# The second matrix of an attention + ELU layer: seven products of halves in its last three blocks

## The chip, the cores and the metric

The kernel runs on one core of one Trainium2 chip. The metric is the device time in microseconds (us) of one execution. The times given are the median of several runs and their lowest and highest; the profile is of one more execution, taken by the hardware profiler.

## The reference

Attention on two scales comes first, and then a two-layer block with an ELU between the layers:

```python
# q, k, v: (8, 8, 576, 64) = batch, heads, sequence, head size
out_up    = np.repeat(attention over q, k, v averaged over 4 positions, 4)
out_local = attention over q, k, v with the mask abs(i - j) < 4
x = (out_up + out_local).transpose(0, 2, 1, 3).reshape(4608, 512)
...
h = x @ w_in                                   # (4608, 512) @ (512, 2048)
g = np.where(h > 0, h, np.exp(np.minimum(h, 0)) - 1)
return g @ w_out                               # (4608, 2048) @ (2048, 512), float32
```

Inputs and output are float32; the operands of the matmuls are fp16, the sums in PSUM float32.

## The kernel before, in words

**Blocks and batches.** The 4608 tokens are cut into nine blocks `t` of 512 (`TBLK`); the attention runs over eight batches `b` of 576 tokens, four pairs of heads `j` in each. Block 6 holds tokens of batches 5 and 6, block 7 tokens of batches 6 and 7 (64 of the last), block 8 the rest of batch 7. The attention of the last batch is computed while blocks 5 and 6 run in the first layer.

**First layer.** `mm1(t, fc)` makes one of 16 pieces of 128 hidden columns: four matmuls of 128x128 weights by 512 tokens into a PSUM buffer `hp` (two buffers), an exponential on ScalarE into `e`, then two instructions on VectorE: a TENSOR_SCALAR in place on `e` (minimum with 1, minus 1) and a SCALAR_TENSOR_TENSOR that adds max(`hp`, 0) and writes the piece of `gt`. `gt` has two buffers, each [128, 16, 512].

**Second layer.** `mm2(t, i)`, 16 steps: for each 128 tokens, 16 matmuls (four per step) of a 128x128 piece of `gt` as weights by 512 columns of `WO` into a PSUM buffer `op`; after the fourth step a copy on ScalarE into `os` and a DMA to the output. The last 128 tokens are done in two pieces, 384 and 128 columns.

**Attention.** `pair_transposes(b, j)`: transposes on TensorE, a copy to `qt` on ScalarE, and `sums`: on GpSimd two additions, `t` and then `qd` (queries summed over four positions). `pair_scores` needs `qd`. `normalise(b, j, lg)`: two multiplications on VectorE into `ln` (two buffers), and one addition per block on GpSimd into `xt(t)`, the input of `mm1`. Before each pair GpSimd casts q, k and v.

**Order.** It is written out by hand: every piece of work is put into a list by `at(time, function, ...)`; the list is sorted by time and issued in that order, and each engine works through its own instructions in the order of issue. The times are numbers in tables in units of one step. `mm1_at(t, i)` gives step i of block t's first layer; from block 3 on `mm2_at(t, i)` is `mm1_at(t + 1, 0) + 0.5 + i`, so each step of the first layer of a block is followed by one step of the second layer of the block before, and after the last step of block 8 the second layer of block 8 stands alone. `LAST` holds the places of the last batch's attention, relative to the start of block 7.

**Memory.** All SBUF tiles belong to one pool `sb` that lives to the end.

## Time and profile before

| | us |
|---|---|
| median of 3 runs (lowest to highest) | 351.59 (348.52 to 353.46) |
| span of the profiled execution, its own time | 353.6 |
| block 6: first matmul of its first layer to that of block 7 | 249.15 to 281.46 |
| block 7: to the first matmul of block 8 | 281.46 to 309.09 |
| block 8's first layer, to its last matmul's end | 309.09 to 335.85 |
| the matmuls behind it | 335.85 to 350.73 |

The profile gives the busy time of each engine (PE is TensorE, PEld its weight loads, DVE VectorE, ACT ScalarE, POOL GpSimd, SP the queue of DMAs), and each instruction with its line in the kernel, its start in the span and its length. "x4" stands for four instructions of one kind merged into one row. Behind a "<-" in square brackets stands what ended the idle time of the engine before the row. For a difference of one or two per cent the stretch in which the changed instructions stand has to be read, not the sums over the span.

### The profile page before, as it was taken

The page shows a single profiled execution, that of the slowest core. Times are in us where ns is not written, and L with a number is a line of the kernel's source. Part 1 is how long each engine was busy: PE and PEld are TensorE (multiplying, and loading weights), DVE is VectorE, ACT ScalarE, POOL GpSimd, SP SyncE. Part 2 cuts the span into 40 slices and gives each one's busy share as a digit, 9 for nine tenths or more (in the row PEclk, how much of TensorE's full clock was granted, in tenths as well). Part 3 has the DMA queues.
Part 4 walks back from the last instruction along what each step waited for, and adds up shares of the span by engine and source line. Part 5 has one row for each costly group of instructions (what it writes and reads, how often), then busy time and mean ns, then how long its engine had stood idle before and what let it go on. Part 6 is the DMA issues. An engine that isn't in the chain of part 4 may idle for free.

```text
span 353.6 us, 10486 instructions
## 1 busy us (share of the span) xinstructions
PE 335.8 (95%) x4288; PEld 185.3 (52%) x4288; DVE 236.2 (67%) x466; ACT 180.6 (51%) x312; POOL 160.0 (45%) x298
## 2 busy tenths in 40 slices
PE   8897998899889998899999999999999999999996
PEld 4665784455455544445555555545455544444443
DVE  2316999665878775977797789779756955555510
ACT  3572795256665653466355636663553444444421
POOL 4563458286875841973396449755300600000000
PEclk9998999879989999999999999999999999999999
DMA  9999997899998869898979797953014010010012
GB/s 177 201 209 192 213 208 152 200 213 190 188 185 158 167 139 181 168 190 158 196 150 214 158 214 155 168 131 54 30 35 116 32 59 31 32 52 37 32 59 89
DMA packets 98768, 48.89 MB, mean 138 GB/s; under 512 B 81617, under 2 KB 93217, under 8 KB 98721
## 3 DMA queue, kind: packets, MB, share of 16 engines
q1 hardware_dynamic: 94417, 41.86, 58.7%
q0 software_dynamic: 4064, 6.26, 10.0%
q8 instruction: 33, 0.54, 0.7%
q10 hardware_dynamic: 240, 0.11, 0.2%
q14 instruction: 14, 0.11, 0.1%
HBM read 41.97 MB, written 9.55 MB: 146 GB/s over the span
## 4 chain that ended last, share of the span: by engine, by line
PE 75%; DVE 13%; DMA 6%; issue 3%; ACT 3%; SPq 0%; DVEq 0%; ACTq 0%
PE op L739 31%; PE hp L719 28%; DVE gt L725 4%; DMA rcb<-rd 3%; DVE e L724 3%; DVE ln L671 2%; DMA rd<-rc 2%; PE sc L758 2%; PE tqk L328 2%; PE sc L458 2%; PE lg L602 1%; ACT e L723 1%; PE vs L405 1%; PE lg L622 1%; PE den L518 1%
## 5 line engine op out<-in xcount | busy, mean ns | idle before, releaser
L739 PE MATMUL op<-WO,gt 128*128 128x512 f16 (+2 forms) x592 | 146.0, 375 | 0.5 <-DVE gt L725 0.5
L723 ACT ACTIVATE e<-hp 128x512 f16<-128x512 f32 x144 | 86.2, 599 | 107.1 <-PE hp L719 95.3
L719 PE MATMUL hp<-xt,WI 128*128 128x512 f16 x512 | 133.7, 385 | 1.4 <-DVE gt L725 1.3
L725 DVE SCALAR_TENSOR_TENSOR gt<-hp,e 128x512 f16<-128x512 f32 x144 | 99.6, 692 | 6.4
L724 DVE TENSOR_SCALAR e<-e 128x512 f16<-128x512 f16 x144 | 60.6, 421 | 58.4 <-ACT e L723 58.0
L739 PEld LDWEIGHTS <-gt 128*128 128x128 f16 x592 | 55.4, 98 | 61.7 <-issue 1.6
L719 PEld LDWEIGHTS <-WI 128*128 128x128 f16 x512 | 55.6, 115 | 50.0 <-issue 3.2
L683 POOL TENSOR_TENSOR xt<-ln 128x128 f16<-128x128 f16 (+7 forms) x55 | 36.6, 693 | 56.9 <-DVE ln L671 56.9
L481 ACT ACTIVATE pex<-sc 128x580 f16<-128x580 f32 (+1 forms) x56 | 30.1, 594 | 9.2 <-PE sc L471 8.6
L302 POOL CAST v<-v 128x640 f16<-128x640 f32 (+1 forms) x32 | 23.7, 741 | 20.4 <-DMA v<-in_v_dram 13.6
L394 POOL TENSOR_TENSOR t<-qt 128x288 f32<-128x288 f16 x27 | 18.1, 670 | 31.4 <-ACT qt L358 31.4
L745 ACT COPY os<-op 128x512 f32<-128x512 f32 (+2 forms) x37 | 21.4, 578 | 18.9 <-PE op L739 18.8
L377 DVE TENSOR_REDUCE ke<-kt 128x145 f16<-128x580 f16 x28 | 21.0, 751 | 2.4 <-ACT kt L365 2.4
L358 ACT COPY qt<-tqk 128x576 f16<-128x576 f16 x28 | 17.9, 639 | 8.4 <-PE tqk L328 7.7
L671 DVE TENSOR_TENSOR ln<-lg,rcb 128x580 f16<-128x580 f32 x28 | 21.1, 752 | 0.0
L241 POOL CAST k<-k 96x768 f16<-96x768 f32 x24 | 19.8, 825 | 0.1
L241 POOL CAST q<-q 96x768 f16<-96x768 f32 x24 | 19.6, 818 | 0.0
L698 PE MATMUL hp<-xt,WI 128*128 128x256 f16 x128 | 17.0, 283 | 0.7 <-DVE v L276 0.4
L496 DVE TENSOR_TENSOR pex<-pex,MASK 128x580 f16<-128x580 f16 x28 | 13.6, 486 | 3.0 <-ACT pex L481 2.8
L698 PEld LDWEIGHTS <-WI 128*128 128x128 f16 x128 | 13.3, 116 | 1.9 <-issue 0.8
L396 POOL TENSOR_TENSOR qd<-t 128x144 f16<-128x144 f32 x27 | 12.1, 448 | 2.1
L458 PEld LDWEIGHTS <-kt 64*64 64x64 f16 x560 | 6.9, 109 | 11.2 <-issue 8.6
(113 smaller groups left out, 273.4 us busy)
## 6 DMA issues: line engine op xcount, KB each, us to landing
out_dram<-os SPq DMA_DIRECT2D x35, 256.0 KB, 2.1
v<-in_v_dram SPq DMA_DIRECT2D x111, 80.0 KB, 4.5
q<-in_q_dram SPq DMA_DIRECT2D x25, 288.0 KB, 3.9
...
```

Source lines behind the costliest of these rows:

```text
L241: nc.gpsimd.tensor_copy(out=x[:], in_=src)
L302: nc.gpsimd.tensor_copy(out=v16[:], in_=v32[:].rearrange("p (e c) d -> p c e d", e=2))
L481: nc.scalar.activation(out=s["p"][:, :, a : a + n], in_=g2(sc, a, n), func=AF.Exp, scale=SCALE / 16 if a else SCALE,)
L671: nc.vector.tensor_tensor(out=ln[:, 0 : 2 * WL].rearrange("p (m h u) -> p m h u", h=2, u=WQ), in0=_free(lg[:, 0:1], [[WQ, WM], [512, 2], [ ...
L683: eng.tensor_tensor(out=xt(t)[:, j, t0 - TBLK * t : t1 - TBLK * t], in0=ln[:, a:z], in1=_rep4(ln[:, ga : ga + (z - a) // 4]), op=AB.add,)
L698: nc.tensor.matmul(FS[i][:, 256 * f : 256 * f + 256], w_in(dc, 2 * n + f), xts[0][:, dc, 256 * h : 256 * h + 256], start=(f == dc == 0), s ...
L719: nc.tensor.matmul(hp, w_in(dc, fc), xts[t][:, dc, :], start=(dc == 0), stop=(dc == DMC - 1),)
L723: nc.scalar.activation(out=e, in_=hp, func=AF.Exp)
L724: nc.vector.tensor_scalar(out=e, in0=e, scalar1=1.0, scalar2=-1.0, op0=AB.min, op1=AB.add)
L725: nc.vector.scalar_tensor_tensor(out=to, in0=hp, scalar=0.0, op0=AB.max, in1=e, op1=AB.add)
L739: nc.tensor.matmul(op_[:, a:z], gts[t][:, fc, 128 * tt : 128 * tt + 128], WO[:, fc, a:z], start=(fc == 0), stop=(fc == FCN - 1),)
L745: nc.scalar.copy(out=os_[:, a:z], in_=op_[:, a:z])
```

## The change

For blocks 6, 7 and 8 (`SW = 6`) the second layer is computed in Strassen's form (Winograd's variant). Of `gt`, the tokens are halved (first and last 256) and the hidden columns (first and last 1024), which gives quarters a11, a12, a21, a22; of `WO`, the hidden rows and the output columns, b11 to b22. Seven products of quarters take the place of eight:

- four differences of quarters of `WO`, kept in a tile `T` [128, 4, 8, 256]: `weights_7(n, c)`, 16 subtractions on GpSimd, each of 128x512 elements, once;
- for each block four sums of quarters of `gt`: `sums_7(t, g)`, four groups g of four operations of 128x512 on GpSimd, a group after every fourth step of the first layer (in block 8 the last group is on VectorE). One of them, a11 - a21, is written over a21; the three others go into a tile `S`;
- `product(t, u, n)`, n from 1 to 7, for each unit u of 2 x 128 tokens (128 of the first half and 128 of the last): eight matmuls of 256 columns, each with its own 128x128 weights. Both units together have 112 matmuls of 256 columns, where `mm2` had 64 of 512. Partial results are copied to `sn` by ScalarE, and added on VectorE into `ou` (behind product 4 a [128, 2, 256] addition, behind product 5 one of [128, 256]).

The first layer of these blocks takes the hidden columns in another order (0, 8, 1, 9, ...), so that each group of sums finds its four pieces. In the slots between the steps of blocks 7 and 8 stand products at steps 0 to 5 and 7, and at 8 to 13 and 15: steps 6 and 14 have none behind them. In block 8 all products stand behind the last step.

```diff
-    def mm1(t, fc):
+    def mm1(t, i):
+        fc = i if t < SW else i // 2 + 8 * (i % 2)
...
+    def weights_7(n, c):
+        T, k = W7["T"], slice(2 * c, 2 * c + 2)
+        b11, b12 = WO[:, k, 0:MH], WO[:, k, MH:DM]
...
+        x, y = ((b12, b11), (b22, T[:, 0, k]), (b22, b12), (b21, T[:, 1, k]))[n]
+        nc.gpsimd.tensor_tensor(out=T[:, n, k], in0=x, in1=y, op=AB.subtract)
+    def sums_7(t, g):
...
+        a11, a12, a21, a22 = G[:, k, 0:TH], G[:, l, 0:TH], G[:, k, TH:TBLK], G[:, l, TH:TBLK]
+        eng = nc.vector if (t, g) == (NT - 1, 3) else nc.gpsimd
+        for to, x, y, op in (
+            (S[:, 0, k], a21, a22, AB.add), (a21, a11, a21, AB.subtract),
+            (S[:, 1, k], S[:, 0, k], a11, AB.subtract), (S[:, 2, k], a12, S[:, 1, k], AB.subtract),
+        ):
+            eng.tensor_tensor(out=to, in0=x, in1=y, op=op)
...
+    def product(t, u, n, k0=0, k1=FH):
+        xz, y, sn, ou = unit(t, u)
...
+        to = y[:, 0:MH] if n in (1, 3, 5, 6) else xz[:, 0:MH] if n == 2 else xz[:, MH:DM]
+        for k in range(k0, k1):
+            w, x = (
+                (G[:, k, a], WO[:, k, 0:MH]), (G[:, FH + k, a], WO[:, FH + k, 0:MH]),
+                (S[:, 2, k, a], WO[:, FH + k, MH:DM]), (G[:, FH + k, b], T[:, 3, k]),
+                (S[:, 0, k, a], T[:, 0, k]), (S[:, 1, k, a], T[:, 1, k]), (G[:, k, b], T[:, 2, k]),
+            )[n - 1]
+            nc.tensor.matmul(
+                to, w, x, start=(k == 0 and n in (1, 2)), stop=(k == FH - 1),
...
+        if n in (1, 6, 7):
+            nc.scalar.copy(out=sn[:, {1: 0, 6: 1, 7: 2}[n], :], in_=to)
+        if n == 4:
+            nc.vector.tensor_tensor(
+                out=ou[:, :, 0:MH], in0=xz[:].rearrange("p (c m) -> p c m", c=2), in1=sn[:, 0:2, :],
+                op=AB.add,
+            )
+        if n == 5:
+            nc.vector.tensor_tensor(out=ou[:, 1, MH:DM], in0=to, in1=sn[:, 2, :], op=AB.add)
+            nc.sync.dma_start(out=out[z : z + 128], in_=ou[:, 1, :])
...
+        if n == 3:
+            nc.scalar.copy(out=ou[:, 0, MH:DM], in_=to)
...
-            if 16 * t + i <= 16 * NT - 4:
+            if t < SW:
                 at(mm2_at(t, i), mm2, t, i)
+    at(PLAN[B - 1]["cast"][3] + 0.05, close_feed)
+    at(PLAN[B - 1]["tr"][3] + 0.05, close_turn)
+    for n in range(4):
+        for c in range(4):
+            at(PLAN[B - 1]["cast"][3] + 0.6 + 1.2 * (4 * n + c), weights_7, n, c)
+    for t in range(SW, NT):
+        for g in range(4):
+            at(mm1_at(t, 4 * g + 3) + 0.05, sums_7, t, g)
+        z = mm2_at(t, 0)
+        if t < NT - 1:
+            for u in range(2):
+                for n, x in zip((1, 2, 7, 6, 4, 5, 3), (0, 1, 2, 3, 4, 5, 7)):
+                    at(z + 8 * u + x, product, t, u, n)
+        else:
+            steps = [(u, n, 0, FH - 1) for u in range(2) for n in (1, 2)]
+            steps += [(u, n, FH - 1, FH) for u in range(2) for n in (1, 2)]
+            steps += [(u, n) for u, n in ((0, 7), (0, 6), (1, 7), (1, 6), (0, 4), (0, 5), (1, 4), (1, 5), (0, 3), (1, 3))]
+            for n, x in enumerate(steps):
+                at(z + n, product, t, *x)
```

For room, tiles that only the attention uses go into two pools of their own (`lo` and `tu`), which are closed after the last batch's casts and after its last transposes; `T`, `S`, `sn` and `ou` take their places. A line of the kernel up to the second layer stands six or seven lines further down than before.

How GpSimd's own row of instructions changes is seen at two places. The first lies at the start of block 6, on GpSimd (POOL): the additions into `xt` of batch 6, and `t` and `qd` of the last two pairs of batch 7. Before:

```order
L683 TENSOR_TENSOR xt<-ln 128x128
L683 TENSOR_TENSOR xt<-ln 128x448
L394 TENSOR_TENSOR t_5455<-qt 128x288
L396 TENSOR_TENSOR qd<-t_5455 128x144
L394 TENSOR_TENSOR t_5549<-qt 128x288
L396 TENSOR_TENSOR qd<-t_5549 128x144
```

After, where `w_5276` is the tile `T` of weight differences:

```order
L772 TENSOR_TENSOR w_5276<-WO 128x512
L689 TENSOR_TENSOR xt<-ln 128x128
L689 TENSOR_TENSOR xt<-ln 128x448
L689 TENSOR_TENSOR xt<-ln 128x128
L689 TENSOR_TENSOR xt<-ln 128x448
L772 TENSOR_TENSOR w_5276<-WO 128x512 x2
L400 TENSOR_TENSOR t_5469<-qt 128x288
L402 TENSOR_TENSOR qd<-t_5469 128x144
L772 TENSOR_TENSOR w_5276<-WO 128x512
L772 TENSOR_TENSOR w_5276<-WO,w_5276 128x512
L400 TENSOR_TENSOR t_5565<-qt 128x288
L402 TENSOR_TENSOR qd<-t_5565 128x144
```

One weight difference now stands ahead of the second half of batch 6's additions, two ahead of the first `t` and two ahead of the second.

The second place is the end of block 6, again on GpSimd: from the last pair's `qd` to the additions into `xt` of batch 7, whose 64-wide ones write block 7's input. Before:

```order
L394 TENSOR_TENSOR t_5549<-qt 128x288
L396 TENSOR_TENSOR qd<-t_5549 128x144
L683 TENSOR_TENSOR xt<-ln 128x64
L683 TENSOR_TENSOR xt<-ln 128x512
L683 TENSOR_TENSOR xt<-ln 128x64
L683 TENSOR_TENSOR xt<-ln 128x512
```

After, the last twelve rows up to the second half of these additions (`s_5597` is the tile `S` of block 6):

```order
L772 TENSOR_TENSOR w_5276<-WO 128x512 x2
L772 TENSOR_TENSOR w_5276<-WO,w_5276 128x512
L785 TENSOR_TENSOR s_5597<-gt 128x512
L785 TENSOR_TENSOR gt<-gt 128x2x256
L785 TENSOR_TENSOR s_5597<-s_5597,gt 128x512
L785 TENSOR_TENSOR s_5597<-gt,s_5597 128x512
L689 TENSOR_TENSOR xt<-ln 128x64
L689 TENSOR_TENSOR xt<-ln 128x512
L689 TENSOR_TENSOR xt<-ln 128x64
L689 TENSOR_TENSOR xt<-ln 128x512
L772 TENSOR_TENSOR w_5276<-WO,w_5276 128x512 x2
L689 TENSOR_TENSOR xt<-ln 128x64
```

Between `qd` and the first of these additions stand eight weight differences (two, three and three) and three groups of sums now, each group behind the step of the first layer that it needs; two more differences stand between the two halves of the additions.

The third place is VectorE in block 7, at its steps 4 to 6. Before, only the pairs of the first layer stand there (with the tiles' numbers, since the rows read alike without them):

```order
L724 TENSOR_SCALAR e_6076<-e_6076 128x512
L725 SCALAR_TENSOR_TENSOR gt_6019<-hp_6077,e_6076 128x512
L724 TENSOR_SCALAR e_6090<-e_6090 128x512
L725 SCALAR_TENSOR_TENSOR gt_6019<-hp_6091,e_6090 128x512
L724 TENSOR_SCALAR e_6103<-e_6103 128x512
L725 SCALAR_TENSOR_TENSOR gt_6019<-hp_6104,e_6103 128x512
```

After:

```order
L731 TENSOR_SCALAR e_6148<-e_6148 128x512
L732 SCALAR_TENSOR_TENSOR gt_6067<-hp_6149,e_6148 128x512
L817 TENSOR_TENSOR ou_6080<-xz_6077,sn_6079 128x2x256
L731 TENSOR_SCALAR e_6166<-e_6166 128x512
L732 SCALAR_TENSOR_TENSOR gt_6067<-hp_6167,e_6166 128x512
L822 TENSOR_TENSOR ou_6080<-y_6078,sn_6079 128x256
L731 TENSOR_SCALAR e_6185<-e_6185 128x512
L732 SCALAR_TENSOR_TENSOR gt_6067<-hp_6186,e_6185 128x512
```

The additions of products 4 and 5 now stand behind the pairs of steps 4 and 5.

More of the change, by code (lines that the diff above doesn't have):

```diff
@@ L35 @@
 FLIP = 3
+SW = 6
 I1 = 31
@@ L120, in const @@
     def const(a, name, queue):
-        t = C[name] = sb.tile(list(a.shape), FP16, tag=name, bufs=1, name=name)
+        pool = sb if name in ("ID", "MASK", "IND2", "VR2") else lo
+        t = C[name] = pool.tile(list(a.shape), FP16, tag=name, bufs=1, name=name)
         queue.dma_start(out=t[:], in_=nc.inline_tensor(a, name=name + "c").ap())
+    feed = ctx.enter_context(ExitStack())
+    turn = ctx.enter_context(ExitStack())
+    lo = feed.enter_context(tc.tile_pool(name="lo", bufs=1, side="right"))
+    tu = turn.enter_context(tc.tile_pool(name="tu", bufs=1))
     front = ctx.enter_context(ExitStack())
@@ L175, in load_wo @@
         nc.gpsimd.dma_start(out=WO[:, 4 * n : 4 * n + 4, :], in_=src)
[L177 removed]
+    KD = [lo.tile([128, 2 * KG + 16], FP16, tag=f"kd{i}", bufs=1, name="kd") for i in range(4)]
     KE = [sb.tile([128, 192], FP16, tag=f"ke{i}", bufs=1, name="ke") for i in range(4)]
@@ L391, in sums @@
         else:
-            t2 = sb.tile([128, 2 * SD], FP32, tag="pex", bufs=2, name="t2")
+            t2 = tu.tile([128, 2 * SD], FP32, tag="pex", bufs=2, name="t2")
             at_ = src.rearrange("p (g f) -> p f g", f=2)
@@ L730, in mm2 @@
         tt, part = i // 4, i % 4
-        cols = ((0, DM),)
-        if t == NT - 1 and tt == 3:
-            cols, part = ((0, 384), (384, DM)), 0
-        for a, z in cols:
-            if part == 0:
-                ops[(t, tt)] = bank("misc", "op")
-            op_ = ops[(t, tt)]
-            for fc in range(4 * part, 4 * part + 4 if len(cols) == 1 else FCN):
-                nc.tensor.matmul(
-                    op_[:, a:z], gts[t][:, fc, 128 * tt : 128 * tt + 128], WO[:, fc, a:z],
-                    start=(fc == 0), stop=(fc == FCN - 1),
-                )
-            if part == 3 or len(cols) == 2:
-                os_ = sb.tile([128, DM], FP32, tag="os", bufs=3, name="os")
-                nc.scalar.copy(out=os_[:, a:z], in_=op_[:, a:z])
-                r = TBLK * t + 128 * tt
-                nc.sync.dma_start(out=out[r : r + 128, a:z], in_=os_[:, a:z])
+        if part == 0:
+            ops[(t, tt)] = bank("misc", "op")
@@ new lines, in mm2 @@
+        op_ = ops[(t, tt)]
+        for fc in range(4 * part, 4 * part + 4):
+            nc.tensor.matmul(
+                op_[:], gts[t][:, fc, 128 * tt : 128 * tt + 128], WO[:, fc, :],
+                start=(fc == 0), stop=(fc == FCN - 1),
+            )
+        if part == 3:
+            os_ = sb.tile([128, DM], FP32, tag="os", bufs=3, name="os")
+            nc.scalar.copy(out=os_[:], in_=op_[:])
+            r = TBLK * t + 128 * tt
+            nc.sync.dma_start(out=out[r : r + 128], in_=os_[:])
```

58 lines of the change are left out of this document (45 added, 13 removed).

## The prediction

> Times are microseconds from the start of the span; i counts the 16 steps of a block's first layer, each followed by one step of the second layer of the block before. "Matmul step" is one such group of four matmuls.
>
> **What bounds the kernel now.** The page comes first: which engine is full.
>
> ```profile
> PE 335.8 (95%) x4288; PEld 185.3 (52%) x4288; DVE 236.2 (67%) x466; ACT 180.6 (51%) x312; POOL 160.0 (45%) x298
> ```
>
> An average over stages says little, so the stretches of blocks 6, 7, 8 and of the last second layer were asked for; columns after the length are busy PE, PEld, DVE, ACT, POOL, then the granted clock.
>
> ```profile
> 249.15:281.46 32.31, 32.31 (x391) 16.61 (x390) 22.59 (x46) 15.47 (x26) 6.34 (x10) 1.00 0.20 58
> 281.46:309.09 27.63, 27.63 (x129) 13.49 (x128) 15.87 (x33) 11.91 (x20) 0.20 (x1) 1.00 0.10 39
> 309.09:335.85 26.76, 26.76 (x125) 13.06 (x124) 15.62 (x32) 11.31 (x19) 0.00 (x0) 1.00 0.10 40
> 335.85:353.57 17.72, 14.88 (x85) 7.54 (x83) 1.11 (x3) 3.69 (x7) 0.00 (x0) 1.00 0.20 74
> ```
>
> PE is full in all of them, at full clock; GpSimd is nearly idle (6.34 of 32.31, then nothing), VectorE is busy 22.59 of 32.31 in block 6 and 15.87 of 27.63 in block 7. The chain of work that ended last consists there of matmuls alone, four at a time:
>
> ```profile
> 335.15 0.86 PE hp L719 x4
> 336.02 14.73 PE op L739 x84
> 350.81 0.27 ACT os L745
> ```
>
> So 0.86 per four is 216 ns per matmul of 512 columns, and any matmul taken away shortens the end, unless PE waits for something instead. That something can only be an engine that gets new work: GpSimd or VectorE.
>
> **The change, part by part.**
>
> *Fewer columns.* A block's second layer was 64 matmuls of 512 columns, 64 x 0.216 = 13.8. It becomes 7 products x 2 units x 8 = 112 matmuls of 256 columns, each with its own 128x128 weight load. The first layer of block 0 already runs that form:
>
> ```profile
> 44.26 2.81 PE L698 MATMUL hp<-xt,WI 128*128 128x256 f16 x24
> L698 PE MATMUL hp<-xt,WI 128*128 128x256 f16 x128 | 17.0, 283 | 0.7 <-DVE v L276 0.4 <-DVE gt L725 0.3
> ```
>
> 24 in 2.81, the last of them 0.28 long: (2.81 - 0.28) / 23 = 110 ns, half of 216; weight loads stay hidden there. 112 x 0.110 = 12.3, so 1.5 less per block. This falls in block 7's slots (second layer of block 6), in block 8's, and in the tail. The tail is 84 matmuls, 14.73; it becomes 15 products of 0.88 = 13.2, 1.5 less. The last copy grows from 128 columns to 256, and the last group's sums stand on VectorE:
>
> ```profile
> L745 ACT COPY os<-op 128x512 f32<-128x512 f32 x35 | 20.6, 590 | 16.5 <-PE op L739 16.4
> L496 DVE TENSOR_TENSOR pex<-pex,MASK 128x580 f16<-128x580 f16 x28 | 13.6, 486 | 3.0 <-ACT pex L481 2.8
> ```
>
> The copy goes from 0.27 to some 0.38 (on the line to the 0.59 of 512 columns), so the tail nets **-1.4**. The sums hide: 40 matmuls, 4.4, come first that need none of them (the product before, products 1 and 2 of both units), while the last gt is done 1.85 after the last matmul step (below: 2.71 from its start) and four sums of at most 0.49 end at 3.8. Without that cover up to 3.8 would show.
>
> *GpSimd's new work.* 16 weight differences, and 16 sums per block, each on two inputs of 512 elements. The rows nearest:
>
> ```profile
> L683 POOL TENSOR_TENSOR xt<-ln 128x512 f16<-128x512 f16 x4 | 4.3, 1070 | 0.0
> L394 POOL TENSOR_TENSOR t<-qt 128x288 f32<-128x288 f16 x27 | 18.1, 670 | 31.4 <-ACT qt L358 31.4
> L302 POOL CAST v<-v 128x640 f16<-128x640 f32 x28 | 20.4, 729 | 12.6 <-DMA v<-in_v_dram 12.5
> ```
>
> Two inputs of 512 took 1.07, and 288 elements 0.67, one line whatever the type and stride (0.16 + 1.78 ns per element). The one-input cast is faster: 1.1 ns per element, so some 0.6 for 512 is the other end. I take 1.07, since both two-input rows have it; in a row of them the next starts 1.03 on. The second and fourth sum of a group wait for the one before on their own engine; the pair t, qd below shows that as 0.08 of idle in place of 0.04 of overlap, so a group of four takes 4 x 1.03 + 2 x 0.12 = 4.4. GpSimd runs in order, so what matters is what stands behind this. Its rows in block 6:
>
> ```profile
> 242.01 2.66 POOL L683 TENSOR_TENSOR xt<-ln 128x128 f16<-128x128 f16 x4 [4.89 <-DVE ln L671]
> 245.17 2.66 POOL L683 TENSOR_TENSOR xt<-ln 128x128 f16<-128x128 f16 x4 [0.51 <-DVE ln L671]
> 247.79 0.71 POOL L394 TENSOR_TENSOR t<-qt 128x288 f32<-128x288 f16 x1
> 248.58 0.43 POOL L396 TENSOR_TENSOR qd<-t 128x144 f16<-128x144 f32 x1
> 254.32 0.67 POOL L394 TENSOR_TENSOR t<-qt 128x288 f32<-128x288 f16 x1 [5.31 <-ACT qt L358]
> 274.50 2.66 POOL L683 TENSOR_TENSOR xt<-ln 128x64 f16<-128x64 f16 x4 [18.88 <-DVE ln L671]
> 279.00 2.66 POOL L683 TENSOR_TENSOR xt<-ln 128x64 f16<-128x64 f16 x4 [1.84 <-DVE ln L671]
> ```
>
> and PE's, with the readers of these:
>
> ```profile
> 250.29 0.27 PE L471 MATMUL sc<-qd,ke 64*64 64x144 f16 x8
> 255.08 1.03 PE L719 MATMUL hp<-xt,WI 128*128 128x512 f16 x4
> 263.67 1.06 PE L719 MATMUL hp<-xt,WI 128*128 128x512 f16 x4
> 270.61 1.03 PE L719 MATMUL hp<-xt,WI 128*128 128x512 f16 x4
> 281.46 1.03 PE L719 MATMUL hp<-xt,WI 128*128 128x512 f16 x4
> ```
>
> *First wait.* One difference stands ahead of the xt group of 245.17 and two behind it. The first starts when the group before ends (244.63), so the xt group starts at 245.66, not 245.17: +0.5; two more are +2.06. So t starts at 250.35 and qd is done at 251.6; the scores that read it (250.29) wait **1.4**. Behind them in PE's queue is everything.
>
> *Second wait.* Block 7's first matmul (281.46) needs the xt group of 279.00, its third operation. Follow GpSimd, with all of PE 1.4 later. The t and qd of the last pair come at 254.32 + 1.4 and end at 256.9. Two differences: 259.0. Sums of group 0 need gt of step 3, whose time from the start of its matmuls is read here:
>
> ```profile
> 256.77 0.29 DVE L724 TENSOR_SCALAR e<-e 128x512 f16<-128x512 f16 x1 [0.71 <-ACT e L723]
> 257.10 0.69 DVE L725 SCALAR_TENSOR_TENSOR gt<-hp,e 128x512 f16<-128x512 f32 x1
> ```
>
> Step 3 started at 255.08 and its gt was done at 257.79, 2.71 later. With 1.4: 259.2. Sums to 263.6, three differences to 266.7, sums of group 1 (step 7: 263.67 + 2.71 + 1.4 = 267.8) to 272.2, three differences to 275.3, sums of group 2 (step 11: 274.7, ready) to 279.7, the first xt group to 282.3, two differences to 284.4, then 64, 512 and 64 elements, 1.6: **286.0**. PE would be there at 281.46 + 1.4 = 282.9, so it waits **3.1**. Bounds: 0, with sums at 0.6 (then every group waits for its gt, and both waits vanish), and 4, if VectorE's turns at the shared port cost GpSimd 0.05 each.
>
> *VectorE in blocks 7 and 8.* Here a lock comes in:
>
> ```profile
> 279.25 1.07 POOL L683 TENSOR_TENSOR xt<-ln 128x512 f16<-128x512 f16 x1
> 279.72 0.75 DVE L724 TENSOR_SCALAR e<-e 128x512 f16<-128x512 f16 x1
> ```
>
> The same TENSOR_SCALAR that took 0.29 at 256.77 took 0.75 here, to 0.15 after GpSimd's operation ended at 280.32. The SCALAR_TENSOR_TENSOR behind it keeps 0.69 in either case. What a late gt does to PE is shown by
>
> ```profile
> 245.89 0.75 DVE L724 TENSOR_SCALAR e<-e 128x512 f16<-128x512 f16 x1
> 246.68 0.69 DVE L725 SCALAR_TENSOR_TENSOR gt<-hp,e 128x512 f16<-128x512 f32 x1
> 247.43 1.02 PE L719 MATMUL hp<-xt,WI 128*128 128x512 f16 x4
> ```
>
> where the matmul step waits until the buffer of two steps earlier is read (247.37). In ordinary slots that buffer has four groups of 0.86, 3.45, and needs 2.71, so 0.46 to 0.75 of lock fits. But seven products fill eight slots: none stands between steps 6 and 7, nor between 14 and 15, and there only three groups, 2.60, are left. From the start of step 3 as zero: its gt is done at 2.7, and the four sums run 2.8-3.9, 3.9-5.0, 5.0-6.0, 6.1-7.2. The TENSOR_SCALAR of step 4 (due at 3.4) ends at 4.0, its partner at 4.7; the add of product 4, from PSUM, follows:
>
> ```profile
> L671 DVE TENSOR_TENSOR ln<-lg,rcb 128x580 f16<-128x580 f32 x28 | 21.1, 752 | 0.0
> ```
>
> 580 elements took 0.75, so 512 take 0.68: 5.35. The TENSOR_SCALAR of step 5 then lies in the third sum and ends at 6.2, its partner at 6.9. Step 7 could start at 6.08 and starts at 6.95: **0.9**. Without the lock it would be 0.15; both ends are kept, 0.9 is taken. Two such places per block, two blocks: 2 x (-1.5 + 2 x 0.9) = **+0.6**. The reduced work there is given back.
>
> *At nothing:* ScalarE copies eight pieces of 0.38 per block, 3.0, for four of 0.59; it is busy 11.9 of 27.6. SyncE sends as many bytes. The pools that move issue nothing.
>
> **Sum.** 1.4 + 3.1 + 0.6 - 1.4 = +3.7 on the profiled 353.6, that is 357.3. The profiled execution is 2.0 above the median of the three times shown (351.59); the difference is taken over, and the forecast is **355.3**.
>
> **Rivals.**
>
> *The clock falls.* Full idle of 3.1 may cost more than itself.
>
> ```profile
> 27.17:30.58 3.41, 1.73 (x48) 0.97 (x46) 2.53 (x3) 0.68 (x2) 1.49 (x3) 1.00 1.24 188
> 30.58:34.00 3.42, 3.42 (x46) 2.67 (x43) 1.33 (x3) 0.76 (x1) 0.00 (x0) 0.50 1.28 191
> 139.81:143.22 3.41, 1.92 (x61) 1.33 (x62) 3.34 (x7) 0.00 (x0) 3.15 (x5) 1.00 1.35 206
> 143.22:146.64 3.42, 3.18 (x20) 1.58 (x19) 3.35 (x9) 2.09 (x4) 3.23 (x8) 1.00 0.46 101
> ```
>
> After 1.7 idle of 3.41 the next stretch had half the clock; after 1.5 idle of 3.41 it had not. A wait of 3.1 leaves one such stretch at least half idle. Half a clock for 3.41 on a full PE costs 1.7: 357.0. The Trainium skill, "TensorE: Matmul & The Clock Gate", section "What's actually happening", lets the clock fall only after at least one idle window of about 3.4 us; by that the forecast stays as it is, while the stretch at 27.17, half busy, fell all the same, so the trace speaks for the rival about as much as against.
>
> *GpSimd keeps up* (the other side: faster). If plain operands side by side go at the cast's rate, 0.6, qd is hardly late, all sums of block 6 wait for their gt, the xt group is in time, and the lock ends earlier (0.25 at each of four places): 2 x (-1.5 + 0.5) - 1.4 = -3.4, 348.2. Between 0.6 and 1.07 the balance crosses zero near 0.83 per operation. For it: no row has two plain halves as inputs. Against: two rows of different stride and type lie on one line.
>
> *The gap closes without the lock:* TENSOR_SCALAR comes between sums; 4 x 0.15 in place of 3.6: 352.3.
>
> *VectorE fills up in block 6.* 16 TENSOR_SCALARs, each 0.46 longer, make 22.6 into 30 of 32.3; bunched with the outputs' multiplications they would make PE wait as at 247.43, some 4 more: 359.3.
>
> *Matmul pace.* The products' weights come from tiles written a moment before, half as many columns per load.
>
> ```profile
> L739 PEld LDWEIGHTS <-gt 128*128 128x128 f16 x592 | 55.4, 98 | 61.7 <-issue 1.6
> ```
>
> A load takes 98 ns. If a third of it showed, 143 ns per product matmul, a block's 112 would take 16.0, 2.2 more than now in place of 1.5 less: 3 x 3.7 = 11 above the forecast, 366. Block 0's stream at 110 ns is against it. The Trainium skill, "TensorE: Matmul & The Clock Gate", section "Back-to-back issue gap", gives for streams of loads and matmuls about 131 ns at 512 columns and 81 at 128, so not in proportion; by an estimate between these, 98 at 256, the products would lose 2.6 per block. The trace's 216 and 110 do not bear that out.
>
> **How the numbers follow.** Forecast 0.38; clock 0.26; GpSimd keeps up 0.17; gap without lock 0.10; VectorE full 0.07; pace 0.02. 347.5 to 359.0 leaves out a third of the fastest case, most of the two slowest, and a tail of the clock's: under 2 in 10. A measurement here tells about 2%, 7.0, from no change: faster than 344.6 has 0.01, slower than 358.6 has 0.12, between them 0.87.
>
> **What would show it.** Products of 0.88 in the chain; the scores of block 6's first step waiting for qd on GpSimd, over 1; block 7's first matmul waiting for xt on GpSimd, about 3, then a granted clock of 0.5 or not; TENSOR_SCALAR at 0.6 or more in blocks 7 and 8, and step 7 and 15 waiting for gt, 0.9 each. It is wrong if GpSimd's new operations take under 0.85, or if 256 columns from gt or from the sums take more than 110 ns.

## The result, and the profile after

| | before | after |
|---|---|---|
| median (lowest to highest) | 352.52 (348.52 to 355.44, 4 runs) | 364.81 (362.74 to 366.91, 4 runs) |
| ratio to before, 95% interval | | 1.0377 [1.0304, 1.045] |
| span of the profiled execution | 353.57 | 363.35 |
| first matmul of block 6 to the end | 104.42 | 113.99 |

The changed kernel is 3.8% slower; 355.3 was forecast, at most 359.0. Here and below, medians and ranges are of all executions, while ratios leave out those that took over 1.5% longer than the fastest of their kernel. The stretches of the profiled execution, cut at the same places as in the prediction (block 6, 7, 8, tail; the columns are the same):

```profile
249.36:287.51 38.15, 32.67 (x392) 16.68 (x391) 28.09 (x46) 16.14 (x27) 34.55 (x36) 0.99 0.19 56
287.51:318.92 31.41, 29.34 (x177) 18.94 (x177) 22.23 (x36) 12.16 (x23) 21.64 (x20) 0.91 0.07 25
318.92:346.97 28.05, 25.81 (x171) 17.37 (x169) 22.43 (x36) 11.94 (x23) 18.29 (x16) 1.00 0.08 30
346.97:363.35 16.38, 13.25 (x121) 11.63 (x119) 5.16 (x11) 3.85 (x10) 0.00 (x0) 1.00 0.27 97
```

Against before, block 6 is 5.84 longer, block 7 3.78, block 8 1.29, and the tail 1.34 shorter: together +9.57. GpSimd, 6.34 busy in block 6 before, is busy 34.55 of 38.15. What TensorE waits for from there to the end (us in total, times, the longest):

```profile
PE hp L726 <- DVE gt L732: 4.0, 4, 1.1
PE hp L726 <- POOL xt L689: 3.7, 1, 3.7
PE sc L477 <- POOL qd L402: 1.8, 1, 1.8
```

These are the waits of the prediction, and no others above 0.2. The first two places on GpSimd's timeline: the group of `t` and `qd`, and the group of `xt` for block 7.

```profile
245.05 1.15 POOL L772 TENSOR_TENSOR w<-WO 128x512 f16<-128x512 f16 x1
246.16 2.70 POOL L689 TENSOR_TENSOR xt<-ln 128x128 f16<-128x128 f16 x4
248.82 2.31 POOL L772 TENSOR_TENSOR w<-WO 128x512 f16<-128x512 f16 x2
251.09 0.77 POOL L400 TENSOR_TENSOR t<-qt 128x288 f32<-128x288 f16 x1
251.94 0.42 POOL L402 TENSOR_TENSOR qd<-t 128x144 f16<-128x144 f32 x1
...
282.28 2.60 POOL L689 TENSOR_TENSOR xt<-ln 128x64 f16<-128x64 f16 x4
284.84 2.31 POOL L772 TENSOR_TENSOR w<-WO,w 128x512 f16<-128x512 f16 x2
287.11 2.64 POOL L689 TENSOR_TENSOR xt<-ln 128x64 f16<-128x64 f16 x4
```

And the readers on TensorE:

```profile
252.42 0.29 PE L477 MATMUL sc<-qd,ke 64*64 64x144 f16 x8 [1.75 <-POOL qd L402]
287.50 1.86 PE L726 MATMUL hp<-xt,WI 128*128 128x512 f16 x4 [3.73 <-POOL xt L689]
```

The scores stand 3.06 behind the start of block 6 (252.42 less 249.36), before 1.14: 1.9 lost there. Of the other 3.9 of block 6 the wait for `xt` is 3.73. In the second row the four matmuls take 1.86 and not 1.03: behind the wait the granted clock is half. In the traces the clock changes at instants that lie whole multiples of 3.41 apart (in the kernel before at 30.58, 34.00, 68.13, 74.96, 102.26 and 105.68), so stretches of that length were asked for; the last column but two is the clock.

```profile
282.97:286.38 3.41, 0.81 (x4) 0.19 (x2) 2.41 (x6) 1.16 (x2) 3.41 (x5) 1.00 0.21 77
286.38:289.80 3.42, 2.29 (x7) 1.06 (x8) 1.61 (x3) 0.39 (x1) 3.42 (x6) 0.51 0.00 0
289.80:293.21 3.41, 3.41 (x13) 1.76 (x12) 1.67 (x2) 0.96 (x3) 3.33 (x3) 0.50 0.00 0
```

TensorE is idle 2.60 of the first stretch, and the two that follow have half the clock. 2.29 + 3.41 of work at half the clock is 2.9 lost, all of it in block 7.

The groups of GpSimd and VectorE that carried the sum (the VectorE row is of blocks 7 and 8, where before it was 297 ns in the mean):

```profile
L785 POOL TENSOR_TENSOR s<-gt 128x512 f16<-128x512 f16 x11 | 12.8, 1165 | 18.8 <-DVE gt L732 12.4 <-PE hp L726 5.3 <-issue 1.1
L772 POOL TENSOR_TENSOR w<-WO 128x512 f16<-128x512 f16 x8 | 9.3, 1173 | 0.0
L689 POOL TENSOR_TENSOR xt<-ln 128x512 f16<-128x512 f16 x4 | 4.3, 1063 | 0.0
L731 DVE TENSOR_SCALAR e<-e 128x512 f16<-128x512 f16 x32 | 20.8, 648 | 13.6 <-ACT e L730 13.6
```

An operation on two plain inputs takes 1.15 to 1.17, not the 1.07 of the `xt` row. One of the four places without a product, on VectorE, GpSimd and TensorE:

```profile
329.19 0.68 DVE L817 TENSOR_TENSOR ou<-xz,sn 128x512 f32<-128x512 f32 x1
329.79 1.11 DVE L731 TENSOR_SCALAR e<-e 128x512 f16<-128x512 f16 x1
330.93 0.69 DVE L732 SCALAR_TENSOR_TENSOR gt<-hp,e 128x512 f16<-128x512 f32 x1
...
329.58 1.16 POOL L785 TENSOR_TENSOR s<-s,gt 128x512 f16<-128x512 f16 x1
...
331.67 1.02 PE L726 MATMUL hp<-xt,WI 128*128 128x512 f16 x4 [1.05 <-DVE gt L732]
```

The TENSOR_SCALAR that starts at 329.79 lasts until GpSimd's operation of 329.58 is over (330.74, it ends at 330.90); its partner ends at 331.62, and the matmul step starts at 331.67.

So from block 6 on the two profiled executions lie 9.6 apart, while the medians lie 12.3 apart. Some 3 had to be found ahead of block 6, where the change issues nothing. These two traces don't show it: block 6 starts at 249.15 and at 249.36. Single traces can't: up to there the kernels of experiments 1, 2, 4 and 8 are the changed kernel, and their block 6 starts at 247.34, 245.18, 251.72 and 250.57; and the span of the trace before, 353.57, is near the top of the 346.7 to 353.8 on record for that kernel.

### The profile page after: what moved, and what is told of

Read it like the earlier page. It is cut to its first block, busy times and chain, and to the rows that moved or that the text cites. A ratio compares the mean times of both kernels' runs of the same rounds, so it can differ in the third digit from the quotient of the medians.

```text
span 363.3 us, 10854 instructions
## 1 busy us (share of the span) xinstructions
PE 335.0 (92%) x4416; PEld 198.9 (55%) x4416; DVE 259.0 (71%) x482; ACT 182.1 (50%) x323; POOL 227.9 (63%) x358
## 2 busy tenths in 40 slices
DMA packets 98770, 48.91 MB, mean 135 GB/s; under 512 B 81617, under 2 KB 93217, under 8 KB 98721
## 3 DMA queue, kind: packets, MB, share of 16 engines
q1 hardware_dynamic: 94417, 41.86, 62.4%
## 4 chain that ended last, share of the span: by engine, by line
PE 55%; DVE 14%; POOL 12%; DMA 9%; ACT 4%; issue 3%; SPq 2%; DVEq 0%; POOLq 0%; ACTq 0%
PE hp L726 19%; PE op L742 13%; PE y L807 5%; DMA rcb<-rd 5%; DVE e L731 5%; DVE gt L732 4%; POOL w L772 4%; DMA rd<-rc 3%; POOL s L785 3%; PE hp L704 3%; ACT e L730 2%; POOL xt L689 2%; PE sc L840 2%; PE xz L807 2%; DVE ln L677 2%
## 5 line engine op out<-in xcount | busy, mean ns | idle before, releaser
L726 PE MATMUL hp<-xt,WI 128*128 128x512 f16 x512 | 135.5, 389 | 9.4 <-DVE gt L732 5.3
L731 DVE TENSOR_SCALAR e<-e 128x512 f16<-128x512 f16 x144 | 76.5, 531 | 45.4 <-ACT e L730 44.9
L742 PE MATMUL op<-WO,gt 128*128 128x512 f16 x384 | 99.3, 382 | 0.5 <-DVE gt L732 0.5
L726 PEld LDWEIGHTS <-WI 128*128 128x128 f16 x512 | 55.6, 115 | 54.4 <-issue 10.4
L487 ACT ACTIVATE pex<-sc 128x580 f16<-128x580 f32 (+1 forms) x56 | 30.1, 593 | 9.6 <-PE sc L477 9.6
L785 POOL TENSOR_TENSOR s<-gt 128x512 f16<-128x512 f16 x11 | 12.8, 1165 | 18.8 <-DVE gt L732 12.4
L748 ACT COPY os<-op 128x512 f32<-128x512 f32 x24 | 14.2, 590 | 5.4 <-PE op L742 5.3
L807 PEld LDWEIGHTS <-s 128*128 128x128 f16 x144 | 14.1, 98 | 4.0
```

What stands on the lines that cost most here:

```text
L487: nc.scalar.activation(out=s["p"][:, :, a : a + n], in_=g2(sc, a, n), func=AF.Exp, scale=SCALE / 16 if a else SCALE,)
L726: nc.tensor.matmul(hp, w_in(dc, fc), xts[t][:, dc, :], start=(dc == 0), stop=(dc == DMC - 1),)
L731: nc.vector.tensor_scalar(out=e, in0=e, scalar1=1.0, scalar2=-1.0, op0=AB.min, op1=AB.add)
L742: nc.tensor.matmul(op_[:], gts[t][:, fc, 128 * tt : 128 * tt + 128], WO[:, fc, :], start=(fc == 0), stop=(fc == FCN - 1),)
L807: nc.tensor.matmul(to, w, x, start=(k == 0 and n in (1, 2)), stop=(k == FH - 1), skip_group_check=n > 2,)
```

## The experiments

The theory from here on (A): the loss is made of the two waits for GpSimd, the half clock behind the second, and the four places where VectorE is late because of GpSimd's operations. Ratios are to the kernel before, measured on the same chip.

**1. Products spread evenly.** Seven product matmuls in each slot, in the same order, so that no slot is empty.

```diff
-                for n, x in zip((1, 2, 7, 6, 4, 5, 3), (0, 1, 2, 3, 4, 5, 7)):
-                    at(z + 8 * u + x, product, t, u, n)
+            for m in range(0, 112, 7):
+                    ...
+                    at(z + m // 7, product, t, u, n, k0, k0 + n_k)
```

> The 112 product matmuls of a block are spread evenly, 7 behind each step of the first layer, so that no two steps stand next to each other; all else as in the changed kernel. Theory A (a TENSOR_SCALAR held by GpSimd's sums makes the matmul step behind an empty slot wait about 1.0, twice in each of blocks 7 and 8): these four waits go, blocks 7 and 8 get shorter by 3.5 to 4 together, about 361 us median, with the two waits on GpSimd in block 6 (1.8 and 3.7) and the low clock as they were. Rival B (VectorE's total work is the bound in these blocks, since each held TENSOR_SCALAR costs it 0.35): the waits only move to other steps, under 1 us gained.

Measured: 374.07 (372.15 to 376.82), ratio 1.0646 [1.0577, 1.0715], slower than the changed kernel. Its longest waits from block 6 on, beside the two for GpSimd, which are as they were:

```profile
PE y L807 <- DVE ou L822: 9.1, 4, 2.3
```

Both sides missed. The four waits of 1.0 for `gt` are gone, but product 3 now follows product 5 at once and writes the PSUM buffer `y` that VectorE's add of product 5 (L822) still has to read: four waits of 2.3. The empty slot stood there for that add. It cost 1.0 and hid 2.3. Behind two of these four waits the clock fell to half as well (it was 0.50 from 319 to 321 and from 336 to 338).

**2. No sums in blocks 7 and 8.** The sums of quarters of `gt` are left out there; the products read block 6's sums in their place, so that their number and size stay.

```diff
-        G, S, T = gts[t], S7.get(t), W7["T"]
+        G, S, T = gts[t], S7.get(SW), W7["T"]
...
-        for g in range(4):
+        for g in range(4 if t == SW else 0):
             at(mm1_at(t, 4 * g + 3) + 0.05, sums_7, t, g)
```

> Leaves out the sums of blocks 7 and 8 (their products read block 6's sums), with the empty slots as in the changed kernel. Theory A: without GpSimd beside them the TENSOR_SCALARs take 0.29 to 0.30 in those blocks, the wait behind an empty slot falls from 1.0 to 0.15-0.2, blocks 7 and 8 together 3.2 to 3.5 shorter, about 361.4 us. Rival (the wait comes from the additions behind products 4 and 5, which stay, and not from the lock): the waits stay above 0.6, under 1.5 gained.

Measured: 360.71 (355.91 to 362.4), ratio 1.0215 [1.0132, 1.0298]. Blocks 7 and 8:

```profile
283.31:312.25 28.94, 28.93 (x176) 18.81 (x176) 18.87 (x36) 12.16 (x23) 7.93 (x8) 0.91 0.07 27
312.25:337.74 25.49, 25.48 (x170) 17.38 (x169) 16.80 (x35) 11.94 (x23) 0.00 (x0) 1.00 0.09 33
```

TensorE has no idle time left in either, with the empty slots and the adds of products 4 and 5 as they were. So the late `gt` comes from GpSimd's operations beside VectorE, and not from the adds. The two blocks are 5.0 shorter than in the changed kernel, more than the 3.2 to 3.5 expected. Block 8 is 1.27 below before's 26.76 here, where 1.5 was reckoned; with the sums it is 1.29 above. The sums cost 2.56 in block 8 and 2.47 in block 7, more than the seven products save.

**3. Weight differences on VectorE.**

```diff
-        nc.gpsimd.tensor_tensor(out=T[:, n, k], in0=x, in1=y, op=AB.subtract)
+        nc.vector.tensor_tensor(out=T[:, n, k], in0=x, in1=y, op=AB.subtract)
```

> The 16 weight differences at the same places in the order, but on VectorE; the sums stay on GpSimd. Theory A (GpSimd's queue, 18 us of differences in it, is what makes qd and xt late): the scores' wait for qd vanishes, block 7's first matmul waits under 0.5 in place of 3.7, and the clock stays at full speed behind it: 1.8 + 3.4 + 2.9 = 8 less, about 357 us, if VectorE's 16 x 0.5 = 8 hide in its idle time in blocks 5 and 6 (10 of 32 idle). Rival B (VectorE is nearly full beside a busy GpSimd): matmul steps in block 6 wait for gt instead and 3 or more of the 8 are given back, 360 or above.

Measured: 360.16 (358.0 to 360.77), ratio 1.0231 [1.0173, 1.0288]. Its block 6:

```profile
247.80:283.59 35.79, 32.81 (x392) 16.57 (x390) 33.28 (x59) 16.07 (x27) 21.07 (x22) 1.00 0.20 59
```

and the only wait of TensorE from there to the end:

```profile
PE hp L726 <- DVE gt L732: 8.1, 8, 2.1
```

Both waits for GpSimd vanish, so the weight differences make them. Of the 5.8 lost in block 6, 2.4 came back: VectorE is now busy 33.28 of 35.79, and four new waits for `gt` take 4.1 (the other 4.0 are the four of blocks 7 and 8). The clock did not stay up either. Behind the longest of the new waits, 2.12, which left TensorE busy for 1.29 of its stretch of 3.41, it was half for one stretch, at the start of block 7, which takes 30.29 at 0.94 in the mean. So the time is rival B's: a nearly full VectorE takes the place of GpSimd.

**4. Work in place of the idle time.** Sixteen matmuls of 512 columns that nobody reads, ahead of block 7's first matmul.

```diff
+    def warm():
+        y = unit(SW, 0)[1]
+        for _ in range(16):
+            nc.tensor.matmul(y[:, 512:1024], WI[:, 0, 0:128], WI[:, 0, 0:512], start=True, stop=True)
+
+    at(mm1_at(SW + 1, 0) - 0.01, warm)
```

> The changed kernel with 16 matmuls of 512 columns more, 3.5 us, on a piece of PSUM that nobody reads, issued just ahead of block 7's first matmul, where TensorE otherwise idles 3.7 for xt. Theory A with the clock (the low clock behind that wait comes from the idle time and costs 2.9): the wait's end stays where it is, the clock behind it stays at full speed, 2.5 to 3 gained, about 362 us. Rival (the low clock comes at fixed places or by chance, as in the early part of the span): still a stretch of 0.5 near 286-293, no gain, or a loss of up to 0.5.

Measured: 363.32 (361.96 to 366.04), ratio 1.0344 [1.0281, 1.0407]. Blocks 6 and 7:

```profile
251.72:290.48 38.76, 36.13 (x408) 18.14 (x406) 28.59 (x46) 16.14 (x27) 35.16 (x36) 1.00 0.18 55
290.48:319.50 29.02, 26.68 (x177) 18.13 (x176) 22.25 (x35) 12.16 (x23) 21.05 (x20) 1.00 0.07 27
```

With work in the idle time the clock stays at 1.00, and block 7 takes 29.02 in place of 31.41; block 6 pays 0.6 for the extra matmuls. The half clock is a consequence of the idle time, and is worth 2.4 here. The medians agree in size (1.5 below the changed kernel), but the intervals of the two ratios overlap; it is the trace that shows it.

**5. The same wait in the kernel before.** Six plain subtractions on GpSimd between the two halves of batch 7's additions into `xt`, nothing else.

```diff
+    def busy():
+        nc.gpsimd.tensor_tensor(out=Z[:], in0=WO[:, 0, :], in1=WO[:, 1, :], op=AB.subtract)
+
+    for n in range(6):
+        at(mm1_at(7, 0) - 3.5 + 0.01 * n, busy)
```

> The kernel before, with six plain subtractions of 128x512 on GpSimd (two quarters of WO into the unused Z) between the two halves of batch 7's additions into xt, which makes block 7's first matmul wait: 6 x 1.16 = 7 on a group that was to start at 279.0 and end its third operation at about 281.2, so a wait of some 6 to 7 minus the slack, 4 to 7. Theory A (an idle time of 3.7 or more at this place brings half a clock for 6.8, worth 2.9 to 3.4 behind it): half-clock stretches of 3.4 to 6.8 within 5 of the wait's end, the whole 7 to 9 slower, 359 to 361. Rival G (the half clock in the changed kernel came from elsewhere, as from the products' stream): clock stays at 1.0 and only the wait shows, 4 to 6 slower.

Measured: 357.23 (353.57 to 357.93), ratio 1.0152 [1.0086, 1.0217]. The reader of `xt` on its timeline:

```profile
282.54 1.87 PE L719 MATMUL hp<-xt,WI 128*128 128x512 f16 x4 [3.08 <-POOL xt L683]
```

and the clock stretches around it:

```profile
278.78:282.20 3.42, 0.68 (x4) 0.21 (x2) 1.84 (x3) 1.04 (x2) 3.26 (x4) 1.00 0.20 77
282.20:285.61 3.41, 3.07 (x8) 1.08 (x8) 0.43 (x2) 0.60 (x1) 2.60 (x5) 0.50 0.00 0
285.61:289.02 3.41, 3.41 (x18) 1.62 (x17) 1.54 (x3) 1.06 (x2) 0.00 (x0) 1.00 0.00 0
```

The wait was 3.1, less than expected, and one stretch of half the clock followed, not two. By its time alone this would be rival G, 4 to 6 slower, but the clock did fall. Block 6 took 35.56 (before 32.31) and block 7 29.12 (before 27.63): 4.7 for a wait of 3.1. So the wait and the clock need nothing of the seven products; late GpSimd work at this place is enough. The Trainium skill, "TensorE: Matmul & The Clock Gate", section "What's actually happening", asks for at least one idle window of about 3.4 us before the clock falls; here it fell behind a stretch that was busy for 0.68 of 3.42, and in the changed kernel behind one busy for 0.81, so the measurement decides against that wording.

**6. The pools alone.** `SW = 9` and no weight differences: no products, no sums, only the tiles in their new pools (and the last 128 tokens in one piece, 0.8 longer at the end: 18.52 from the start of the last second layer on its own, before 17.72). This tests what the expectations call rival C: that the missing 3 come from the moved memory.

```diff
-SW = 6
+SW = 9
...
-            at(PLAN[B - 1]["cast"][3] + 0.6 + 1.2 * (4 * n + c), weights_7, n, c)
+            pass
```

> Only the memory pools are moved and closed as in the changed kernel; there are no products, weight differences or sums, all nine blocks have the old second layer, and the last 128 tokens are done in one piece (0.3 longer at the end). Theory A: no difference from before, about 352. Rival C (the pools shift casts, transposes or their transfers ahead of block 6): about 3 slower, 355, with the first matmul of block 6 some 3 later in the trace than before's 249.15 minus 2 to 5.

Measured: 356.64 (352.31 to 364.96), ratio 1.0116 [1.005, 1.0183], so 4.1 slower by the ratio (times 352), 3.3 without the end, with an interval from 1.0 to 5.6: rival C, not theory A. Its trace is of the execution of 364.96 and is read for its packets alone. Up to the last 128 tokens every engine issues the same instructions in the same order as in the kernel before; only addresses differ. What differs in the page is the row of the queue that loads q, k and v, and also carries the output (packets, MB, and the time of its packets as a share of 16 engines' span). In the kernel before:

```profile
q1 hardware_dynamic: 94417, 41.86, 58.7%
```

In the changed kernel, with the row above that shows how full DMA is in 40 slices of the span (tenths):

```profile
DMA  8999997999998979997999799660032001011013
...
q1 hardware_dynamic: 94417, 41.86, 62.4%
```

The share times 16 times the span by the count gives the mean time of a packet: 35.2 ns before (58.7% of 353.6), 38.4 after (62.4% of 363.3). Every trace with moved pools so far had 38.0 to 39.2; the only other one without, that of experiment 5, 34.9.

**7. What the addresses do.** By the page 81617 of the 98768 packets of the kernel before are under 512 bytes; the loads, into the tiles `v32`, `q32` and `k32`, are more than half of the bytes of this queue. In the kernel before these tiles start 160, 128 and 128 bytes behind a multiple of 256; in the moved pools all three start 224 behind one. Unused tiles shift them, and with them, in the kernel before, two small tiles (`ID` and `Z`). In the kernel before, first to 224:

```diff
+    sb.tile([128, 32], FP16, tag="pad_v", bufs=1, name="pad_v")
     V00 = sb.tile([KW, 2 * NB, D], FP32, tag="v32", bufs=3, name="v32")
...
+        sb.tile([128, 16], FP16, tag="pad_q", bufs=1, name="pad_q")
         load_qk(0, 0)
+        sb.tile([128, 80], FP16, tag="pad_k", bufs=1, name="pad_k")
```

> The kernel before with three unused tiles that shift the tiles into which v, q and k are loaded: from 160 (v32) and 128 (q32, k32) behind a multiple of 256 bytes to 224, as the changed kernel's moved pools leave them; all else stays where it was, modulo 256. In every run with moved pools the packets of the load queue took 38.0 to 39.1 ns (share x 16 x span / 94417), in the two traces without 34.9 and 35.2. Theory H (the offset does it, and the longer packets are the 3 or so that the moved pools cost ahead of block 6): 38 to 39 ns per packet, 354 to 355 us beside 351.7. Rival I (it is the moving itself: another side, other neighbours, or chance): 35 ns, 351.7.

and with other sizes of the same tiles (48, 16 and 64) to 0:

> The kernel before with v32, q32 and k32 shifted to multiples of 256 bytes. Theory H in its form by 256 (a piece of 256 bytes that starts elsewhere takes a second transaction): packets of about 28 ns, estimated from 35.0 at 13 and 12 beats and 38.5 at 15, so 1.5 ns per beat and 8 beats at zero; the front, whose DMA is busy 8 to 9 tenths, gets 2 to 5 shorter, 347 to 350. In its form by 64 (v32 alone was off a multiple of 64): 32 to 33 ns, 349 to 351. Rival I: 35 ns, 351.7.

In the kernel of experiment 6, 32 bytes bring them from 224 to 192:

```diff
         load_qk(0, 0)
+        lo.tile([128, 16], FP16, tag="pad", bufs=1, name="pad")
```

> The kernel with the moved pools alone (no products), with v32, q32 and k32 brought from 224 to 192 behind a multiple of 256 by an unused tile of 32 bytes: a multiple of 64, but not of 128 or 256. Form by 64: packets at or under 35 ns and a time of 351 to 352.5 (the one-piece end costs 0.8). Form by 256 (14 beats in place of 15): about 37 ns, 354 to 355.

The row of the load queue in the kernel before with its tiles at 224:

```profile
q1 hardware_dynamic: 94417, 41.86, 64.7%
```

with its tiles at 0:

```profile
q1 hardware_dynamic: 94417, 41.86, 52.1%
```

and in the kernel with the moved pools alone, at 192:

```profile
q1 hardware_dynamic: 94273, 41.86, 61.4%
```

| start of `v32` / `q32`, `k32`, bytes behind a multiple of 256 | span | ns per packet | median | ratio to before |
|---|---|---|---|---|
| 0 / 0 | 346.8 | 30.6 | 350.3 | 0.995 [0.9916, 0.9984] |
| 160 / 128 (before) | 353.6 | 35.2 | 352.12 | 1 |
| 192 / 192 (moved pools, end 0.8 longer) | 348.2 | 36.3 | 352.86 | 1.0011 [0.9969, 1.0053] |
| 224 / 224 | 352.5 | 38.6 | 354.49 | 1.0088 [1.0051, 1.0124] |

The span is that of the one profiled execution and enters the time of a packet alone. Theory H held: a shift of 64 and 96 bytes, with nothing else, makes the packets as long as in the moved pools and costs 0.88%, 3.1 us [1.8, 4.4]. In the moved pools, 32 bytes back took 1.0% off again (1.0116 to 1.0011), though these two intervals overlap. The packets grow with the distance; the 75761 of 256 bytes among them took 21.9, 26.6, 27.4 and 30.1 ns in the order of the table. At 192, a multiple of 64, they are longer than before, which speaks against the form by 64, but the time there came out near that form (its interval is 351.0 to 354.0) and not at 354 to 355, so which of the two forms the time follows stays open. At zero they were 30.6, not the 28 reckoned, and the gain of 0.5% (1.8 us) came out just short of the 2 to 5 expected, though its interval excludes no change. The Trainium skill, "DMA: Bandwidth & Descriptors", section "How a descriptor splits into AXI transactions", says that a transaction has to start at a multiple of 256 bytes, so that a piece starting behind one also pays for the bytes ahead of it; the order of the four rows agrees with that. The Trainium skill words this for reads; here it is the address written that was moved.

**8. The products spread in another order.** In the changed kernel, seven matmuls in each slot as in experiment 1, but product 3 of the first unit four products behind its product 5, and product 5 of the second unit ahead of its product 4 (with its output DMA, which moves behind product 4).

```diff
...
+            seq = [(0, n) for n in (1, 2, 7, 6, 4, 5)] + [(1, n) for n in (1, 2, 7, 6)] + [(0, 3), (1, 5), (1, 4), (1, 3)]
+            for m in range(0, 112, 7):
+                    ...
+                    at(z + m // 7, product, t, u, n, k0, k0 + n_k)
```

> The changed kernel with its 112 product matmuls spread seven to a step in blocks 7 and 8, and product 3 of the first unit moved four products behind its product 5, product 5 of the second unit ahead of its product 4. Theory A (the empty slots cost one late gt each, four times 0.98 to 1.05; spreading in the first trial failed only because product 3 then stood directly behind product 5 and waited 2.3 for VectorE's read of y): the four waits vanish and nothing takes their place, block 7 about 29 (the half clock of 2.9 remains), block 8 about 25.5 to 26, the whole about 4 less than the changed kernel, 360. Rival F (VectorE, with its TENSOR_SCALARs at 0.64, can't keep up with seven matmuls of every slot, wherever the products stand): waits of about 1 elsewhere, less than 1 gained, 363 or more.

Measured: 363.98 (362.37 to 364.9), ratio 1.036 [1.0301, 1.0419], the same as the changed kernel's 1.0377. Its block 8:

```profile
319.17:346.50 27.33, 26.08 (x171) 17.48 (x170) 22.13 (x36) 11.33 (x24) 18.51 (x16) 1.00 0.11 39
```

and TensorE's waits from the end of block 6 on:

```profile
PE hp L726 <- POOL xt L689: 4.2, 2, 3.7
PE y L807 <- DVE ou L824: 1.6, 2, 0.8
PE hp L726 <- DVE gt L732: 0.8, 3, 0.3
```

Block 8 gains 0.7 (27.33 in place of 28.05), not 2 to 2.5. The four waits of 1.0 shrink to shorter ones, but a wait for the add of product 5 (0.8 in each block) remains. In both orders tried beside GpSimd's sums the wait moved rather than went away: rival F, mostly.

**9. Two blocks, early differences.** `SW = 7`, the weight differences all behind the last `qd`, the order of experiment 8:

```diff
-SW = 6
+SW = 7
...
-            at(PLAN[B - 1]["cast"][3] + 0.6 + 1.2 * (4 * n + c), weights_7, n, c)
+            at(PLAN[B - 1]["tr"][3] + 0.06 + 0.01 * (4 * n + c), weights_7, n, c)
```

> Seven products for blocks 7 and 8 only (SW = 7); block 6's second layer is the old one. All 16 weight differences stand right behind the last pair's qd on GpSimd (16 x 1.16 = 18.6, from about 253 to 272, ahead of the xt additions that were at 274.5 in the kernel before), and block 8's slots hold seven product matmuls each, in an order in which product 3 of the first unit comes four products after its product 5. Theory A (what the change loses are the two waits for GpSimd, the idle time's half clock and the empty slots): no wait for qd or xt, no half clock behind 142, no wait at steps 7 and 15; block 6 about 32.3 to 33, block 7 27.6 to 28, block 8 about 25.5, tail 16.4, together 2.5 less than before in the back part: about 349 where the kernel before has 351.6. Rival C (the moved memory pools cost some 3 ahead of block 6): the same back part, but 352 to 353. Rival D (VectorE fills up in block 6, since 16 differences lengthen its TENSOR_SCALARs by 0.46): waits for gt of 2 to 4 in block 6, 351 to 353.

Measured: 354.81 (353.43 to 358.18), ratio 1.0125 [1.0066, 1.0185]. Blocks 6 to 8 and the tail:

```profile
248.00:280.42 32.42, 32.42 (x391) 16.46 (x390) 26.20 (x46) 15.45 (x26) 24.66 (x26) 1.00 0.20 58
280.42:308.69 28.27, 27.97 (x129) 13.51 (x129) 20.35 (x33) 11.90 (x20) 14.23 (x13) 1.00 0.10 38
308.69:336.07 27.38, 25.92 (x170) 17.44 (x169) 21.78 (x36) 11.51 (x23) 18.43 (x16) 1.00 0.08 29
336.07:352.35 16.28, 13.15 (x120) 11.54 (x118) 5.34 (x11) 3.85 (x10) 0.00 (x0) 1.00 0.27 98
```

No wait for GpSimd, no half clock behind block 6, and block 6 as short as before (rival D, a full VectorE, didn't come: 26.20 busy of 32.42). But block 7 gives 0.64 away and block 8 0.62, both by the sums beside VectorE, and the tail brings 1.44: 104.35 to the end, where the kernel before has 104.42. Theory A had the waits right and the gain wrong; rival C had the loss ahead of block 6 right, but the gain that was to offset it didn't come.

**10. The same with the loads at multiples of 256 bytes,** by one more tile in the pool `lo`:

```diff
+        lo.tile([128, 112], FP16, tag="pad", bufs=1, name="pad")
```

> Seven products in blocks 7 and 8 alone, weight differences early, seven product matmuls in each slot (as in the trial of two blocks), and v32, q32, k32 at multiples of 256 bytes. Theory H: what the moved pools cost is gone, so 354.8 less 3.4, less what the better offset gives (2 to 5 by the form by 256): 346 to 350, below the kernel before. Rival I: 354 to 355 as without the shift. The back part stays as it was in that trial: blocks 6, 7, 8 and tail 32.4, 28.3, 27.4, 16.3.

Measured: 350.4 (348.47 to 354.22), ratio 0.9974 [0.994, 1.0008], packets of 30.9 ns, the stretches from block 6 on within 0.01 of experiment 9. The time is just above the 346 to 350 expected. The shift brought 4.4 by the medians and 5.3 by the ratios, so rival I is out; that the kernel comes out below the kernel before, as theory H had it, is not shown, since the interval includes 1. So of the two versions at zero, the kernel before with shifted tiles (350.3) and this one (350.4), neither is the better: what remains of the seven products, done where they fit, is nothing that can be measured.

## Why the prediction was wrong, by its own steps

| term | predicted | measured | from |
|---|---|---|---|
| first wait, scores for `qd` | +1.4 | +1.9 | scores 3.06 behind block 6's start, 1.14 before |
| second wait, `xt` | +3.1 | +3.9 | the rest of block 6's +5.84; 3.73 of it is the wait |
| clock behind it | 0 (rival: 1.7) | +2.4 to 2.9 | experiment 4; the two stretches |
| blocks 7 and 8 otherwise | +0.6 | +2.2 to 2.7 | 3.78 + 1.29 less the clock |
| tail | -1.4 | -1.34 | 17.72 and 16.38 |
| ahead of block 6 | 0 | +3.1 [1.8, 4.4] | tiles at 224 in the kernel before |
| sum | +3.7 | +12.7, by the middle of each term | medians: +12.3 |

- **The step that failed outright** is "The pools that move issue nothing", costed at nothing. They issue nothing, but they move the tiles that the loads write, from 160 and 128 to 224 bytes behind a multiple of 256, which cost 3.1 in experiment 7; and the loads fill the front: DMA is busy 7 to 9 tenths, mostly 9, in the first 25 of 40 slices (the row in experiment 6). A quarter of the loss stood in a sentence that asked what a pool issues, not what its address does.
- **GpSimd's duration was mis-sized.** 1.07 was taken from the `xt` row because both of its operands seemed like two inputs of 512; plain operands take 1.15 to 1.17 (measured in the changed kernel). The two waits came out 0.5 and 0.8 above their terms. Three differences stand ahead of `qd`, 0.09 each or 0.27 of the first 0.5; the rest of both was not split further. The bound named for the second wait, 4, held, though no run singles out the 0.05 per operation that it was made of.
- **The likeliest case was the wrong one between forecast and first rival.** "The clock falls" came true, and its price was too low, 1.7 in place of 2.4 to 2.9: it reckoned one stretch, but the wait ended inside the second, and two ran at half the clock. Nor does "A wait of 3.1 leaves one such stretch at least half idle" follow: split evenly it leaves 1.55 in each of two, between the 1.49 that had kept the clock and the 1.68 that had not. And the two pairs of stretches shown there were not all; two more of the same trace speak for the rival:

```profile
64.72:68.13 3.41, 2.60 (x76) 1.85 (x75) 2.65 (x6) 0.20 (x1) 0.77 (x1) 1.00 0.85 215
68.13:71.54 3.41, 3.00 (x64) 1.67 (x61) 1.83 (x4) 0.71 (x1) 2.15 (x5) 0.50 0.97 212
98.85:102.26 3.41, 2.95 (x56) 2.01 (x56) 3.28 (x6) 1.85 (x4) 2.67 (x6) 1.00 1.43 127
102.26:105.68 3.42, 3.32 (x40) 1.52 (x40) 2.31 (x5) 1.62 (x4) 1.94 (x3) 0.50 1.28 228
```

Here the clock fell behind stretches idle for 0.81 and 0.46 only. The rival deserved more than 0.26; with its two stretches the forecast would have been 358.2.

- **Blocks 7 and 8.** The mechanism was right to the instruction: the four places, the TENSOR_SCALAR that ends with GpSimd's operation, the add behind it. The wait was 1.0 in place of 0.9. The rest of the difference is the saving, 1.27 per block as experiment 2 shows, not 1.5, and smaller waits and stretched matmuls elsewhere: in block 8, 2.24 of idle time in four pieces (two of 1.0, two of 0.1) and 0.33 more of busy TensorE than without sums, so 2.24 + 0.33 - 1.27 = 1.30.
- **The tail** was right, and so was the pace: products of 256 columns ran at 110 ns from written tiles as from constants (seven in a row, 0.77 apart at their starts). The rival on that pace falls, as do "GpSimd keeps up" and the gap without a lock. "VectorE fills up" didn't come in block 6 of the changed kernel (28.09 of 38.15), but did as soon as the weight differences were put on it.
